# Batch 1's queries turned by the DMA crossbar instead of TensorE, with batch 2's loads and the work around them re-ordered

## The chip, the cores and the metric

The kernel runs on one core of a Trainium2 chip. The metric is device time in microseconds (us), lower is better. Before the change it is 317.51 us, the median of 3 runs (317.42 to 317.64). A profile's own span, from the first to the last instruction, is 1.8 to 2.1 us shorter than the device time of the same run. All timed runs told of here are of the fast state, except two single runs whose state cannot be told (slow1 and slow2).

## The reference

Linear attention over 8 batches, then a SwiGLU block over all 4,608 tokens:

```python
# q, k, v: (batch 8, heads 8, seq 576, dim 64), float32
q_s = softmax(q, over dim);  k_s = softmax(k, over seq)
kv  = einsum('bhsd,bhse->bhde', k_s, v)
x   = einsum('bhsd,bhde->bhse', q_s, kv)      # -> (4608, 512)
g, val = x @ w_gate, x @ w_val                 # (512, 1536) each
out = (g * sigmoid(g) * val) @ w_out           # (1536, 512)
```

## The kernel before

The SwiGLU block fills TensorE; the attention of batch b+1 is slipped in between its products. Batch 1 is the exception: its attention stands alone between the twelve units of batch 0 (`m_unit`, 576 tokens) and the first chunk of the main loop (448 tokens). I call the stretch from batch 0's first output product to the first output product of the next chunk **the passage**. Every head group G (two in a batch) goes through the same steps: load q, k, v; Exp on ScalarE; row sums, reciprocal and multiply on VectorE (`norm_sum`, `norm_mul`); a transpose of the normalised q; K^T V with the sums of k (`kv_...`), scaled (`scale_...`); and x = q^T times that (`x_...`), copied into `xt`, which the units read.

```python
    ld = ctx.enter_context(tc.tile_pool(name="ld", bufs=3))     # 3 buffers each of q, k, v
    ff = ctx.enter_context(tc.tile_pool(name="ff", bufs=3))     # 3 buffers of Silu's result
    psp = ctx.enter_context(tc.tile_pool(name="psp", bufs=8, space=bass.MemoryType.PSUM))
    # ... cut
    def turn_pe(b, G, i):          # by TensorE: 5 + 4 transposes into one PSUM bank each
        # ... cut
            nc.tensor.transpose(out=tp[:, j * 128:(j + 1) * 128], in_=s["qs"][:, t, :], identity=ident)
    def turn_out(b, G, i, eng):    # and a copy out of PSUM
        # ... cut
    def turn_dma(b, G):            # by the DMA crossbar; batches 2 to 7 use it
        s = st[b, G]
        qt = s["qt"] = at.tile([128, T, 128], BF16, tag="qt", name="qt")
        nc.sync.dma_start_transpose(out=qt, in_=s["qs"].rearrange("p t c -> p (t c)"))
    # ... cut
    def m_unit(c0, n, m, by_part=False):     # gate and value products, Silu, product
        # ... cut: two PSUM banks, 4 + 4 matmuls
            nc.scalar.activation(out=sg[:, 0:w_], in_=g_ps[:, 0:w_], func=AF.Silu)
            nc.vector.tensor_mul(hr[:, m, r:r + w_], sg[:, 0:w_], u_ps[:, 0:w_])
    # ... cut
        load_batch(1, w_dma[-3], by_group=True)
        load_batch(2)
        for m in range(MT):
            m_unit(0, S, m, by_part=(m == 0))
        exp_of("q", 1, 0); exp_of("k", 1, 0); exp_of("q", 1, 1)
        cast_v(1, 0); cast_v(1, 1)                      # GpSimd
        norm_sum(1, 0); norm_mul(1, 0); norm_sum(1, 1)  # VectorE
        o_out(0, o_mm(0), nc.scalar); o_out(1, o_mm(1), nc.scalar)
        exp_of("k", 1, 1)
        # turn, K^T V, scale and x of group 0, then of group 1, round o_mm(2) and o_mm(3)
        # ... cut
        exp_of("q", 2, 0); exp_of("q", 2, 1)
        x_one(1, 1)
        o_out(3, p)
        exp_of("k", 2, 0); exp_of("k", 2, 1)

        for ci, (c0, n) in enumerate(chunks):
            # ... cut: in the first chunk, in front of units 1 to 4: cast, norm_sum,
            # norm_mul and turn_dma of batch 2
                if att and m == 8:
                    kv_both(b)
                    scale_both(b)
                    if b + 1 < B:
                        load_batch(b + 1)
                m_unit(c0, n, m)
                if att and m == 9:
                    x_both(b)
```

(Several calls are put on one line here.) In the traces ScalarE loads a table whenever it goes from Exp to Silu or back (1.28 us each), so an Exp among Silus costs two table loads. And the program has eight PSUM banks (`bufs=8`), handed round among all products: a product waits until the last reader of its bank is done.

The softmax here doesn't subtract the row's maximum and nothing guards it: scores larger than these inputs give would overflow.

Of the kernel before, what the change touches and what calls it, by code (L numbers as in the profile page):

```python
# [15 lines left out]
def kernel(  # L16
# [30 lines left out]
    def bank(name):  # L47
        return psp.tile([128, 512], FP32, tag="ps", name=name)
# [34 lines left out]
    def load_batch(b, after=None, by_group=False):  # L83
        qkv = (("q", q), ("k", k), ("v", v))
        if by_group:
            order = [(w, s, G) for G in range(NG) for w, s in qkv]
        else:
            order = [(w, s, G) for w, s in qkv for G in range(NG)]
        for w, s, G in order:
            load(w, s, b, G, after=after)  # L90
            after = None
# [40 lines left out]
    def norm_sum(b, G, pieces=((0, T),)):  # L132
        s = st[b, G]
        eq2 = s["eq"].rearrange("p t h d -> p (t h) d")
        rs = at.tile([128, 2 * T], FP32, tag="rs", name="rs")
        first = None
        for t0, t1 in pieces:
            i = nc.vector.reduce_sum(  # L138
                out=rs[:, 2 * t0:2 * t1], in_=eq2[:, 2 * t0:2 * t1, :], axis=mybir.AxisListType.X
            )  # L140
            first = first or i
        rr = s["rr"] = at.tile([128, 2 * T], FP32, tag="rr", name="rr")
        nc.vector.reciprocal(out=rr, in_=rs)
        return first

    def norm_mul(b, G, pieces=((0, T),), engs=None):
        s = st[b, G]
        eq2 = s["eq"].rearrange("p t h d -> p (t h) d")
        qs = s["qs"] = at.tile([128, T, 128], BF16, tag="qs", name="qs")
        for (t0, t1), eng in zip(pieces, engs or (nc.vector, nc.vector)):  # L150
            n = 2 * (t1 - t0)
            eng.tensor_mul(  # L152
                qs[:, t0:t1, :].rearrange("p t (h d) -> p (t h) d", d=64),
                eq2[:, 2 * t0:2 * t1, :],
                s["rr"][:, 2 * t0:2 * t1].to_broadcast([128, n, 64]),
            )
# [126 lines left out]



    def m_unit(c0, n, m, by_part=False):
        ms = slice(m * 128, (m + 1) * 128)
        parts = [(c0, n)] if n <= 512 else [(c0, 320), (c0 + 320, n - 320)]
        gu = []
        for nm in ("g_ps", "u_ps"):  # L290
            ps = [bank(nm) for _ in parts]
            gu.append(ps)
        steps = [(a, kk, i) for a in range(2) for kk in range(KT) for i in range(len(parts))]
        if by_part:
            steps.sort(key=lambda a: (a[2], a[0], a[1]))
        for a, kk, i in steps:
            c, w_ = parts[i]
            nc.tensor.matmul(  # L298
                out=gu[a][i][:, 0:w_], lhsT=(wg, wv)[a][:, kk, ms], rhs=xt[:, kk, c:c + w_],
                start=(kk == 0), stop=(kk == KT - 1),  # L300
            )
        for g_ps, u_ps, (c, w_) in zip(gu[0], gu[1], parts):
            r = c % RING
            sg = ff.tile([128, 512], BF16, tag="sg", name="sg")
            nc.scalar.activation(out=sg[:, 0:w_], in_=g_ps[:, 0:w_], func=AF.Silu)  # L305
            nc.vector.tensor_mul(hr[:, m, r:r + w_], sg[:, 0:w_], u_ps[:, 0:w_])  # L306
# [8 lines left out]
            )  # L315
            engs[half].dma_start(out=dst, in_=o_sb[64 * half:64 * half + 64, c0:c1])

    def o_mm(j):
        o_ps = bank("o_ps")
        r0 = (j * 128) % RING  # L320
        for m in range(MT):
            nc.tensor.matmul(  # L322
                out=o_ps, lhsT=hr[:, m, r0:r0 + 128], rhs=wo[:, m, :],
                start=(m == 0), stop=(m == MT - 1),
            )
        return o_ps
# [26 lines left out]
    with tc.manual_schedule():  # L353
# [98 lines left out]
        x_out(0, 1, 1, xp1[1], (nc.scalar, nc.vector))  # L452

        load_batch(1, w_dma[-3], by_group=True)
        load_batch(2)

        for m in range(MT):
            m_unit(0, S, m, by_part=(m == 0))
# [5 lines left out]
        cast_v(1, 1)  # L464
        norm_sum(1, 0)
        norm_mul(1, 0)
        norm_sum(1, 1)
        o_out(0, o_mm(0), nc.scalar)
        o_out(1, o_mm(1), nc.scalar)
        exp_of("k", 1, 1)  # L470
        turn_pe(1, 0, 0)
        turn_pe(1, 0, 1)
        turn_out(1, 0, 0, nc.scalar)
        turn_out(1, 0, 1, nc.scalar)
        kv_one(1, 0)
        scale_one(1, 0, (nc.vector, nc.vector))
        norm_mul(1, 1)
        p = o_mm(2)
        x_one(1, 0)
        o_out(2, p)  # L480
        turn_pe(1, 1, 0)
        turn_pe(1, 1, 1)
        turn_out(1, 1, 0, nc.scalar)
        turn_out(1, 1, 1, nc.scalar)
        kv_one(1, 1)
        scale_one(1, 1, (nc.vector, nc.vector))
        p = o_mm(3)
        exp_of("q", 2, 0)
        exp_of("q", 2, 1)
        x_one(1, 1)  # L490
        o_out(3, p)
        exp_of("k", 2, 0)
        exp_of("k", 2, 1)


        chunks = [(S, 448)] + [(c, 512) for c in range(1024, n_tok, 512)]
        for ci, (c0, n) in enumerate(chunks):
            b = ci + 2
            jo = 4 * ci
            att = b < B  # L500
            final = ci == len(chunks) - 1
            for m in range(MT):
                if ci == 0:
                    if m == 1:
                        cast_v(b, 0)
                        cast_v(b, 1)
                        norm_sum(b, 0)
                    elif m == 2:
                        norm_mul(b, 0)
                        turn_dma(b, 0)  # L510
                    elif m == 3:
                        norm_sum(b, 1)
                    elif m == 4:
                        norm_mul(b, 1)
                        turn_dma(b, 1)
                elif m == 3:
                    if att:
                        exp_of("q", b, 0)
                        exp_of("q", b, 1)
                        norm_sum(b, 0)  # L520
                    o_unit(jo)
                    if att:
                        norm_mul(b, 0)
                        turn_dma(b, 0)
                    o_unit(jo + 1)
                    if att:
                        norm_sum(b, 1)
                elif m == 4 and att:
                    norm_mul(b, 1)
                    turn_dma(b, 1)  # L530
                elif m == 7:
                    if att:
                        exp_of("k", b, 0)
                        exp_of("k", b, 1)
                        cast_v(b, 0)
                        cast_v(b, 1)
                    o_unit(jo + 2)
                    if not final:
                        o_unit(jo + 3)
                if att and m == 8:  # L540
                    kv_both(b)
                    scale_both(b)
                    if b + 1 < B:
                        load_batch(b + 1)
                m_unit(c0, n, m)
                if att and m == 9:
                    x_both(b)
        o_unit(jo + 3)
# [34 lines left out]
```

## Time and profile before

| 317.51 us, profiled span 316.0 us | us |
|---|---|
| TensorE busy in the whole span | 304.7 (96%) |
| the passage, 39.19 to 79.09 | 39.90, TensorE busy 39.20 |
| rest of the program after the passage | 236.89 |

The page's line of busy time, and the first line of the chain that ended last:

```profile
...
PE 304.7 (96%) x1865; PEld 152.0 (48%) x1894; DVE 163.2 (52%) x277; ACT 147.6 (47%) x218; POOL 28.0 (9%) x35
...
PE 88%; DMA 4%; DVE 3%; ACT 2%; issue 1%; POOL 1%; SPq 0%; DVEq 0%
...
```

TensorE is the limit. The busy time of each engine in the passage (busy us, then the number of instructions, for each engine; granted TensorE clock, DMA share and rate at the end):

```profile
...
core 0: us, PE busy (x) PEld busy (x) DVE busy (x) ACT busy (x) POOL busy (x), PEclk, DMA share, GB/s
39.19:79.09 39.90, 39.20 (x289) 19.80 (x291) 27.59 (x49) 24.92 (x39) 5.29 (x5) 1.00 0.80 276
...
```

TensorE's timeline in the passage (start, length, what, how many; in brackets idle time before it and who ended it; lengths overlap a little, so read the starts):

```profile
...
44.62 0.68 PE L166 MATMUL tp<-ident,qs 128*128 128x128 bf16 x9
45.23 0.70 PE L191 MATMUL kv<-vb,ek 64*128 64x129 bf16 x18
...
49.08 0.68 PE L166 MATMUL tp<-ident,qs 128*128 128x128 bf16 x9
49.69 0.70 PE L191 MATMUL kv<-vb,ek 64*128 64x129 bf16 x18
...
53.02 0.44 PE L220 MATMUL xp<-qt,kn 64*64 64x320 bf16 x8
53.39 0.55 PE L298 MATMUL g_ps<-xt,wg 128*128 128x448 bf16 x2
54.14 0.54 PE L298 MATMUL g_ps<-xt,wg 128*128 128x448 bf16 x2 [0.20 <-ACT xt L111]
...
65.96 1.22 PE L191 MATMUL kv<-vb,ek 64*128 64x129 bf16 x36
...
70.25 0.69 PE L267 MATMUL xp<-qt,kn 64*64 64x512 bf16 x16
...
```

The `tp` lines are the 18 transposes that the change removes: from 44.62 to 45.23 and from 49.08 to 49.69, 0.61 us each. The bracket before 54.14 is the first unit waiting for the copy of x. The first unit's steady start is 53.76, the second unit's 55.27 less the period of 1.51. K^T V of batch 2 starts at 65.96 and x of batch 2 at 70.25 without any wait.

ScalarE's timeline of the same stretch:

```profile
...
53.97 2.23 ACT L124 ACTIVATE ek<-k 128x1152 bf16<-128x1152 f32 x2
56.22 1.28 ACT L305 ACT_TABLE_LOAD   x1
57.51 1.42 ACT L305 ACTIVATE sg<-g_ps 128x448 bf16<-128x448 f32 x3
59.26 0.54 ACT L305 ACTIVATE sg<-g_ps 128x448 bf16<-128x448 f32 x1 [0.33 <-PE g_ps L298]
60.84 0.54 ACT L305 ACTIVATE sg<-g_ps 128x448 bf16<-128x448 f32 x1 [1.04 <-DVE hr L306]
62.64 0.54 ACT L305 ACTIVATE sg<-g_ps 128x448 bf16<-128x448 f32 x1 [1.25 <-DVE hr L306]
...
```

All four exponentials of batch 2 are done before the first unit's Silu at 57.51; the sixth Silu starts at 62.64. After that ScalarE stands idle in front of each Silu until VectorE has done a product (`<-DVE hr`), because VectorE alternates these products with the normalisation of batch 2.

### The profile page before, as it was taken

Reading aid. Unit: us, or ns where it says so; the run is one execution under the profiler, and the core shown is the slowest. Engines: PE = TensorE matmul, PEld = TensorE weight load, DVE = VectorE, ACT = ScalarE, POOL = GpSimd, SP = SyncE. Lnnn points to the kernel's source line nnn. Section 1 sums busy time; section 2 is a strip of 40 time slices with the busy share of each in tenths; the row PEclk is TensorE's granted clock in tenths of the full one; section 3 lists DMA queues with packets and bytes.
Section 4 is the critical chain, followed back from the end, with each engine's and each line's share of the span. In section 5 each row is a group of like instructions: output and inputs, shape, how many; then the busy total and the mean of one; then the engine's idle time right before and its main releaser. Section 6 shows DMA issues by size and latency. Waiting matters only on the chain.

```text
span 316.0 us, 4856 instructions
## 1 busy us (share of the span) xinstructions
PE 304.7 (96%) x1865; PEld 152.0 (48%) x1894; DVE 163.2 (52%) x277; ACT 147.6 (47%) x218; POOL 28.0 (9%) x35
## 2 busy tenths in 40 slices
PE   6799999999999999999999999999999999999994
PEld 2477744554444444544454444544454444444443
DVE  3834476685754566455835492639354333423421
ACT  4743488634663465447354637355743113312300
POOL 2930021100200020002000200020000000000000
PEclk9999999999999999999999999999999999999999
DMA  7999999269246806490629253944310202020124
GB/s 269 183 204 207 296 393 391 68 160 364 50 91 179 338 17 128 112 394 11 141 68 352 97 110 66 322 162 103 66 41 0 65 3 66 0 68 3 31 68 102
DMA packets 39304, 45.75 MB, mean 145 GB/s; under 512 B 16368, under 2 KB 23024, under 8 KB 39280
## 3 DMA queue, kind: packets, MB, share of 16 engines
q1 hardware_dynamic: 32480, 39.99, 42.0%
q0 software_dynamic: 6640, 5.31, 10.9%
q8 instruction: 15, 0.25, 0.3%
q10 hardware_dynamic: 160, 0.13, 0.2%
q14 instruction: 9, 0.07, 0.1%
HBM read 37.75 MB, written 9.44 MB: 149 GB/s over the span
## 4 chain that ended last, share of the span: by engine, by line
PE 88%; DMA 4%; DVE 3%; ACT 2%; issue 1%; POOL 1%; SPq 0%; DVEq 0%
PE g_ps L298 29%; PE u_ps L298 29%; PE o_ps L322 25%; PE kv L191 3%; DMA wv<-in_moe_w_val_dram 2%; DMA k<-in_k_dram 2%; DVE rs L138 1%; PE xp L267 1%; DVE qs L152 1%; PE o_ps L342 1%; ACT L124 1%; ACT eq L124 1%; POOL v L361 0%; PE tp L166 0%; POOL v L358 0%
## 5 line engine op out<-in xcount | busy, mean ns | idle before, releaser
L305 ACT ACTIVATE sg<-g_ps 128x512 bf16<-128x512 f32 (+2 forms) x120 | 65.1, 554 | 139.1 <-PE g_ps L298 120.7
L306 DVE TENSOR_TENSOR hr<-sg,u_ps 128x512 bf16<-128x512 bf16 (+2 forms) x120 | 74.5, 630 | 87.8 <-PE u_ps L298 80.4
L298 PE MATMUL g_ps<-xt,wg 128*128 128x512 bf16 (+2 forms) x469 | 110.0, 358 | 1.0 <-ACT xt L111 0.2
L298 PE MATMUL u_ps<-xt,wv 128*128 128x512 bf16 (+2 forms) x468 | 109.8, 357 | 1.2 <-DMA wv<-in_moe_w_val_dram 0.5
L322 PE MATMUL o_ps<-wo,hr 128*128 128x512 bf16 x414 | 93.0, 379 | 0.4 <-issue 0.2
L298 PEld LDWEIGHTS <-wv 128*128 128x128 bf16 x480 | 46.9, 98 | 47.2 <-DMA wv<-in_moe_w_val_dram 0.9
L298 PEld LDWEIGHTS <-wg 128*128 128x128 bf16 x480 | 45.8, 98 | 45.3 <-issue 0.7
L322 PEld LDWEIGHTS <-hr 128*128 128x128 bf16 x420 | 40.9, 98 | 49.1
L113 DVE COPY o_sb<-o_ps 128x512 f32<-128x512 f32 x33 | 22.4, 680 | 39.2 <-PE o_ps L322 37.3
L127 POOL CAST vb<-v 128x1152 bf16<-128x1152 f32 x14 | 16.0, 1146 | 174.3 <-DMA v<-in_v_dram 111.8
L138 DVE TENSOR_REDUCE rs<-eq 128x18 f32<-128x1152 bf16 (+2 forms) x18 | 21.7, 1214 | 13.2 <-ACT eq L124 13.2
L152 DVE TENSOR_TENSOR qs<-eq,rr 128x1152 bf16<-128x1152 bf16 (+2 forms) x18 | 22.1, 1237 | 0.1
L124 ACT ACTIVATE eq<-q 128x1152 bf16<-128x1152 f32 (+2 forms) x18 | 18.1, 1050 | 4.5 <-DMA q<-in_q_dram 4.4
L124 ACT ACTIVATE ek<-k 128x1152 bf16<-128x1152 f32 x16 | 18.0, 1158 | 0.3 <-DMA k<-in_k_dram 0.2
L305 ACT ACT_TABLE_LOAD x12 | 15.4, 1283 | 0.2
L124 ACT ACT_TABLE_LOAD x11 | 14.1, 1283 | 0.2
L388 PE MATMUL idle<-zero 128*128 128x512 bf16 x20 | 6.1, 459 | 3.0 <-DVE rs L138 1.8
L191 PE MATMUL kv<-vb,ek 64*128 64x129 bf16 x252 | 8.7, 217 | 0.0
L191 PEld LDWEIGHTS <-ek 64*128 64x128 bf16 x252 | 7.3, 94 | 2.7 <-ACT sg L305 2.1
L275 ACT CAST xt<-xp 128x512 bf16<-128x512 f32 x12 | 6.4, 588 | 3.6 <-PE xp L267 3.6
L276 DVE CAST xt<-xp 128x512 bf16<-128x512 f32 x12 | 7.7, 683 | 0.0
L347 ACT COPY o_sb<-o_ps 128x128 f32<-128x128 f32 x2 | 0.5, 265 | 13.3 <-DVE o_sb L346 13.3
(46 smaller groups left out, 70.2 us busy)
## 6 DMA issues: line engine op xcount, KB each, us to landing
q<-in_q_dram SPq DMA_DIRECT2D x16, 576.0 KB, 5.6
k<-in_k_dram SPq DMA_DIRECT2D x16, 576.0 KB, 7.3
out_dram<-o_sb SPq DMA_DIRECT2D x70, 128.0 KB, 2.3
v<-in_v_dram SPq DMA_DIRECT2D x14, 576.0 KB, 9.0
wo<-in_moe_w_out_dram POOLq DMA_DIRECT2D x4, 384.0 KB, 16.3
wg<-in_moe_w_gate_dram POOLq DMA_DIRECT2D x2, 384.0 KB, 9.7
wv<-in_moe_w_val_dram POOLq DMA_DIRECT2D x2, 384.0 KB, 10.7
wg<-in_moe_w_gate_dram POOLq DMA_DIRECT2D x1, 512.0 KB, 13.7
```

The source lines that it names most:

```text
L113: eng.tensor_copy(out=out, in_=in_)
L124: nc.scalar.activation(out=e[:, t0:t1], in_=src[:, t0:t1], func=AF.Exp)
L127: nc.gpsimd.tensor_copy(out=vbs[G][:, :, 0:128].rearrange("p t (h d) -> p t h d", d=64), in_=raw["v", b, G].rearrange("p h (t d) -> p t h ...
L138: i = nc.vector.reduce_sum(out=rs[:, 2 * t0:2 * t1], in_=eq2[:, 2 * t0:2 * t1, :], axis=mybir.AxisListType.X)
L152: eng.tensor_mul(qs[:, t0:t1, :].rearrange("p t (h d) -> p (t h) d", d=64), eq2[:, 2 * t0:2 * t1, :], s["rr"][:, 2 * t0:2 * t1].to_broadca ...
L191: nc.tensor.matmul(out=kv[g][:, c:c + 129], lhsT=ek_of(b, G, g, t), rhs=vbs[G][r, t, 0:129], start=(t == 0), stop=(t == T - 1),)
L275: nc.scalar.copy(out=xt[:, 2 * G, c0:c0 + 512], in_=main[G][0])
L276: nc.vector.tensor_copy(out=xt[:, 2 * G + 1, c0:c0 + 512], in_=main[G][1])
L298: nc.tensor.matmul(out=gu[a][i][:, 0:w_], lhsT=(wg, wv)[a][:, kk, ms], rhs=xt[:, kk, c:c + w_], start=(kk == 0), stop=(kk == KT - 1),)
L305: nc.scalar.activation(out=sg[:, 0:w_], in_=g_ps[:, 0:w_], func=AF.Silu)
L306: nc.vector.tensor_mul(hr[:, m, r:r + w_], sg[:, 0:w_], u_ps[:, 0:w_])
L322: nc.tensor.matmul(out=o_ps, lhsT=hr[:, m, r0:r0 + 128], rhs=wo[:, m, :], start=(m == 0), stop=(m == MT - 1),)
```

## The change

Its intent: take the 18 transposes and their four PSUM copies from TensorE and ScalarE, let the crossbar do them in time that K^T V and output products cover, and keep the SyncE queue free for them by issuing batch 2's loads around and behind them instead of far ahead. K^T V and x of batch 1 move apart, half an output product between them; the first unit reads the four blocks of x in two groups so that it can start on the first; and the last exponential of batch 2 moves into the first chunk.

```diff
         load_batch(1, w_dma[-3], by_group=True)
-        load_batch(2)
@@
         norm_mul(1, 0)
+        turn_dma(1, 0)
+        load("q", q, 2, 0)
         norm_sum(1, 1)
+        norm_mul(1, 1)
+        turn_dma(1, 1)
+        load("q", q, 2, 1)
+        for what, src in (("k", k), ("v", v)):
+            for G in range(NG):
+                load(what, src, 2, G)
         o_out(0, o_mm(0), nc.scalar)
         o_out(1, o_mm(1), nc.scalar)
         exp_of("k", 1, 1)
-        turn_pe(1, 0, 0)
-        turn_pe(1, 0, 1)
-        turn_out(1, 0, 0, nc.scalar)
-        turn_out(1, 0, 1, nc.scalar)
         kv_one(1, 0)
-        scale_one(1, 0, (nc.vector, nc.vector))
-        norm_mul(1, 1)
+        scale_one(1, 0, (nc.scalar, nc.scalar))
         p = o_mm(2)
+        kv_one(1, 1)
+        o_out(2, p)
+        scale_one(1, 1, (nc.vector, nc.vector))
+        p = o_mm(3, m1=MT // 2)
+        exp_of("q", 2, 0)
         x_one(1, 0)
-        # ... cut: turn, K^T V, scale of group 1, o_mm(3), exponentials of q
+        o_mm(3, p, m0=MT // 2)
         x_one(1, 1)
         o_out(3, p)
+        exp_of("q", 2, 1)
         exp_of("k", 2, 0)
-        exp_of("k", 2, 1)
@@
                     elif m == 4:
                         norm_mul(b, 1)
                         turn_dma(b, 1)
+                    elif m == 5:
+                        exp_of("k", b, 1)
@@
-                m_unit(c0, n, m)
+                m_unit(c0, n, m, by_group=(ci == 0 and m == 0))
```

More of the change, by code (lines that the diff above doesn't have):

```diff
@@ L282, in x_both, with m_unit @@
             )
-    def m_unit(c0, n, m, by_part=False):
+    def m_unit(c0, n, m, by_part=False, by_group=False):
         ms = slice(m * 128, (m + 1) * 128)
@@ L295, in m_unit @@
             steps.sort(key=lambda a: (a[2], a[0], a[1]))
+        if by_group:
+            steps.sort(key=lambda a: (a[1] // 2, a[0], a[1]))
         for a, kk, i in steps:
@@ L316, in store, with o_mm @@
             engs[half].dma_start(out=dst, in_=o_sb[64 * half:64 * half + 64, c0:c1])
-    def o_mm(j):
-        o_ps = bank("o_ps")
+    def o_mm(j, o_ps=None, m0=0, m1=MT):
+        if o_ps is None:
+            o_ps = bank("o_ps")
         r0 = (j * 128) % RING
-        for m in range(MT):
+        for m in range(m0, m1):
             nc.tensor.matmul(
@@ L470 @@
         exp_of("k", 1, 1)
-        turn_pe(1, 0, 0)
-        turn_pe(1, 0, 1)
-        turn_out(1, 0, 0, nc.scalar)
-        turn_out(1, 0, 1, nc.scalar)
         kv_one(1, 0)
-        scale_one(1, 0, (nc.vector, nc.vector))
-        norm_mul(1, 1)
+        scale_one(1, 0, (nc.scalar, nc.scalar))
         p = o_mm(2)
-        x_one(1, 0)
-        o_out(2, p)
-        turn_pe(1, 1, 0)
-        turn_pe(1, 1, 1)
-        turn_out(1, 1, 0, nc.scalar)
-        turn_out(1, 1, 1, nc.scalar)
-        kv_one(1, 1)
-        scale_one(1, 1, (nc.vector, nc.vector))
-        p = o_mm(3)
-        exp_of("q", 2, 0)
-        exp_of("q", 2, 1)
+        kv_one(1, 1)
[3 more added lines that the diff above has]
+        exp_of("q", 2, 0)
+        x_one(1, 0)
+        o_mm(3, p, m0=MT // 2)
         x_one(1, 1)
         o_out(3, p)
+        exp_of("q", 2, 1)
         exp_of("k", 2, 0)
-        exp_of("k", 2, 1)
         chunks = [(S, 448)] + [(c, 512) for c in range(1024, n_tok, 512)]
```

## The prediction

> **What bounds the kernel now.** TensorE. The page shows it busy 304.7 of 316.0 us (96%), and the chain of waits puts 88% of the span on it; granted clock 0.998. The change touches only 39 to 74 us, the passage from batch 0's twelve units to the first chunk of the main loop. The sums over stretches give TensorE 13.75 of 14.19 us busy in 39.20-53.39 and 20.31 of 20.51 in 53.39-73.90. Little idle time can be won; what can go is work.
>
> **What the change removes** (timeline of TensorE). The 18 transposes of batch 1 and the waits around them: 0.86 us before 45.23 and 0.82 us before 49.69. Also a 0.2-0.3 us hole before the third output product, and about 0.35 us before the first chunk unit (0.2 us of it a wait for ScalarE's copy of x), which the order by group should hide. Together about 2.0 us. ScalarE loses four copies out of PSUM (2.4 us).
>
> **What it adds and moves.** Two crossbar transposes: the two of batch 2 took 1.3 us to issue and 3.3 us to land on a quiet queue. Here the queue is full: from 39 to 55 us the DMA engines are saturated at 390 GB/s and loads land in order of issue, one per 1.5 us (the second v of batch 1 at 46.62). The Trainium skill, "DMA: Bandwidth & Descriptors", section "Queues, rings and completion order", says that descriptors are consumed in ring order on each engine; these landings agree. My estimates: first transpose issued 44.6, behind v, landed about 48.5, in time (needed 49.8). Batch 2's first q load is issued at 46 instead of 36.3 and lands about 50.5 instead of 48.1. Second transpose issued about 48.2, landed 51.6 to 52.3; TensorE wants it at 51.5. The second q load lands about 53.8 instead of 49.7, the first k load about 55.3.
>
> **How much stays.** ScalarE runs the exponential of that first q load ahead of x's copies, so x of the first half is ready only about 52.5 to 52.9. The first chunk unit's steady start moves from 53.76 to about 52.7: 1.0, not 2.0 us. ScalarE then waits for the second q and first k loads, so its first Silu slips from 57.5 to about 57.8. In the first chunk VectorE alternates Silu products with batch 2's normalisation, a chain that starts from that Silu; today batch 2's second transposed tile lands at 69.26 and TensorE uses it at 70.25, 1.0 us of slack. Chain 0.3 later: the gain is capped at about 0.7 us there. The fourth exponential, moved into the chunk, costs ScalarE two more table loads (1.28 us each), mostly in time it spends waiting for VectorE. Later chunks only shift.
>
> **Prediction.** 316.8 us, range 316.0 to 317.9. Faster by over 2%: 0.01; within 2%: 0.97; slower by over 2%: 0.02.
>
> **What would show each step.** Right: no TensorE transposes after 20 us; crossbar transposes issued near 44.6 and 48.2, landing near 48.5 and 52; a TensorE hole under 1 us before the second x product or the first chunk unit, and one of a few tenths before batch 2's x product near 69.5; first Silu near 57.8; after that only a shift of 0.7 us. Wrong: x of batch 1 waiting over 1 us for a transpose; the q load landing after 51.5; or a first Silu before 57.5, which would let 1.0 us or more through.
>
> **What would make it wrong.** Crossbar transposes far slower in a busy queue, or holding up the loads behind them (a loss of 1 to 3 us); loads quicker than I reckon, or PSUM banks dealt out so that TensorE never meets VectorE's chain (a gain of 1.3 to 1.7 us).

## The result, and the profile after

The changed kernel takes 318.57 us (median of 4 runs, 318.07 to 319.35) against 317.57 us of before (317.42 to 318.08). Ratios are the mean time of one kernel's runs over that of the other's runs of the same rounds, so not quite the ratio of these medians: 1.0034, 95% interval 1.0016 to 1.0052. Two later measurements of the same kernel gave 1.0016 (1.0004 to 1.0028) and 1.0039 (0.9999 to 1.0079). Over all 15 runs its median is 318.39 us, so it loses about 0.8 us. I had forecast a gain of 0.7.

The page of the changed kernel (of its fastest run of the first four, 318.07 us):

```profile
...
PE 305.0 (96%) x1848; PEld 151.8 (48%) x1876; DVE 162.1 (51%) x275; ACT 148.7 (47%) x218; POOL 29.3 (9%) x35
...
PE 84%; DMA 7%; DVE 2%; ACT 2%; issue 2%; POOL 2%; SPq 0%; DVEq 0%; ACTq 0%
...
```

The passage after, under the same columns as before:

```profile
...
38.91:79.49 40.58, 38.46 (x271) 18.88 (x272) 26.80 (x47) 26.01 (x39) 6.24 (x5) 1.00 0.91 284
...
```

The work did leave: TensorE is busy 38.46 us in the passage instead of 39.20. But the passage has grown from 39.90 to 40.58 us, so its idle time went from 0.70 to 2.12. After the passage nothing differs (236.78 us against 236.89). Here is TensorE's timeline; each code line has moved by two or three (L298 is now L300, L322 is L325):

```profile
...
44.19 0.70 PE L191 MATMUL kv<-vb,ek 64*128 64x129 bf16 x18
44.81 2.76 PE L325 MATMUL o_ps<-wo,hr 128*128 128x512 bf16 x11
48.30 0.70 PE L191 MATMUL kv<-vb,ek 64*128 64x129 bf16 x18 [0.72 <-POOL vb L127]
48.93 1.47 PE L325 MATMUL o_ps<-wo,hr 128*128 128x512 bf16 x6
50.33 0.44 PE L220 MATMUL xp<-qt,kn 64*64 64x320 bf16 x8
50.70 1.47 PE L325 MATMUL o_ps<-wo,hr 128*128 128x512 bf16 x6
52.10 0.44 PE L220 MATMUL xp<-qt,kn 64*64 64x320 bf16 x8
52.47 0.55 PE L300 MATMUL g_ps<-xt,wg 128*128 128x448 bf16 x2
...
65.39 0.23 PE L191 MATMUL kv<-vb,ek 64*128 64x129 bf16 x1 [0.45 <-DVE hr L308]
66.39 1.21 PE L191 MATMUL kv<-vb,ek 64*128 64x129 bf16 x35 [0.77 <-ACT sg L307]
...
70.66 0.69 PE L267 MATMUL xp<-qt,kn 64*64 64x512 bf16 x16
...
```

Up to 52.47 the change did what it was made for: no transposes, x of both halves without a wait, the first unit steady from its first matmul. (One wait is new: 0.72 us for GpSimd's cast of v, in front of the second K^T V.) Then, in front of K^T V of batch 2, TensorE waits twice. Counted from the start of the passage (39.19 before, 38.91 after):

| us from the passage's start | before | after | difference |
|---|---|---|---|
| first unit, steady | 14.57 | 13.56 | -1.01 |
| first Silu of the chunk | 18.32 | 19.22 | +0.90 |
| K^T V of batch 2, first matmul | 26.77 | 26.48 | -0.29 |
| second matmul of it | 26.78 | 27.47 | +0.70 |
| x of batch 2 | 31.06 | 31.75 | +0.69 |
| end of the passage | 39.90 | 40.58 | +0.68 |

ScalarE's timeline says who was late:

```profile
...
56.83 1.28 ACT L307 ACT_TABLE_LOAD   x1
58.13 1.85 ACT L307 ACTIVATE sg<-g_ps 128x448 bf16<-128x448 f32 x4
61.46 0.54 ACT L307 ACTIVATE sg<-g_ps 128x448 bf16<-128x448 f32 x1 [1.48 <-DVE hr L308]
62.02 1.28 ACT L124 ACT_TABLE_LOAD   x1
63.31 1.16 ACT L124 ACTIVATE ek<-k 128x1152 bf16<-128x1152 f32 x1
64.50 1.28 ACT L307 ACT_TABLE_LOAD   x1
65.79 0.98 ACT L307 ACTIVATE sg<-g_ps 128x448 bf16<-128x448 f32 x2
...
```

The first Silu starts at 58.13; four Silus run until 59.98, a fifth at 61.46. Then come a table load, the moved exponential (63.31) and a table load back, and the sixth Silu cannot start before 65.79. It ends at 66.33, and the second matmul of K^T V starts at 66.39. In the program as built (this is read from the build, not from the trace), K^T V's second accumulator sits in the PSUM bank of the sixth unit's gate product, which this Silu reads, and its first in the bank of the fourth unit's value product, which VectorE's fourth product reads until 65.33; that product is late because its chain starts from the late first Silu.

The landings of the DMAs, from the trace's own records:

| landed at, us | before | after | predicted |
|---|---|---|---|
| v of batch 1, second half | 46.62 | 45.83 | about 46.6 |
| first turned tile | | 48.26 | 48.5 |
| first q of batch 2 | 48.12 | 50.21 | 50.5 |
| second turned tile | | 51.31 | 51.6 to 52.3 |
| second q of batch 2 | 49.68 | 54.13 | 53.8 |
| first k of batch 2 | 51.12 | 55.63 | 55.3 |
| second k of batch 2 | 52.63 | 57.13 | |

### The profile page after: what moved, and what is told of

It is laid out like the page before. It is cut to its first block, busy times and chain, and to the rows that moved or that the text cites. A ratio compares the mean times of both kernels' runs of the same rounds, so it can differ in the third digit from the quotient of the medians.

```text
span 316.3 us, 4822 instructions
## 1 busy us (share of the span) xinstructions
PE 305.0 (96%) x1848; PEld 151.8 (48%) x1876; DVE 162.1 (51%) x275; ACT 148.7 (47%) x218; POOL 29.3 (9%) x35
## 3 DMA queue, kind: packets, MB, share of 16 engines
q1 hardware_dynamic: 34848, 40.58, 43.6%
## 4 chain that ended last, share of the span: by engine, by line
PE 84%; DMA 7%; DVE 2%; ACT 2%; issue 2%; POOL 2%; SPq 0%; DVEq 0%; ACTq 0%
PE g_ps L300 28%; PE u_ps L300 27%; PE o_ps L325 25%; DMA v<-in_v_dram 3%; PE kv L191 2%; DMA wv<-in_moe_w_val_dram 2%; DMA k<-in_k_dram 2%; DVE rs L138 1%; PE xp L267 1%; PE o_ps L345 1%; ACT L124 1%; POOL vb L127 1%; ACT sg L307 0%; POOL v L364 0%; DVE qs L152 0%
## 5 line engine op out<-in xcount | busy, mean ns | idle before, releaser
L300 PE MATMUL g_ps<-xt,wg 128*128 128x512 bf16 (+2 forms) x469 | 110.0, 357 | 0.8 <-issue 0.2
L300 PE MATMUL u_ps<-xt,wv 128*128 128x512 bf16 (+2 forms) x468 | 109.9, 357 | 0.7
L325 PE MATMUL o_ps<-wo,hr 128*128 128x512 bf16 x415 | 93.4, 379 | 0.2
L300 PEld LDWEIGHTS <-wv 128*128 128x128 bf16 x480 | 46.8, 98 | 46.9 <-DMA wv<-in_moe_w_val_dram 0.4
L300 PEld LDWEIGHTS <-wg 128*128 128x128 bf16 x480 | 45.8, 98 | 45.1 <-issue 1.0
L325 PEld LDWEIGHTS <-hr 128*128 128x128 bf16 x420 | 40.9, 98 | 49.1 <-issue 0.2
L127 POOL CAST vb<-v 128x1152 bf16<-128x1152 f32 x14 | 17.3, 1233 | 173.4 <-DMA v<-in_v_dram 133.2
L152 DVE TENSOR_TENSOR qs<-eq,rr 128x1152 bf16<-128x1152 bf16 (+2 forms) x18 | 21.8, 1222 | 0.1
L391 PE MATMUL idle<-zero 128*128 128x512 bf16 x20 | 7.3, 525 | 3.2 <-DVE rs L138 2.0
L350 ACT COPY o_sb<-o_ps 128x128 f32<-128x128 f32 x2 | 0.5, 265 | 13.3 <-DVE o_sb L349 13.3
```

The source lines that it names most:

```text
L127: nc.gpsimd.tensor_copy(out=vbs[G][:, :, 0:128].rearrange("p t (h d) -> p t h d", d=64), in_=raw["v", b, G].rearrange("p h (t d) -> p t h ...
L152: eng.tensor_mul(qs[:, t0:t1, :].rearrange("p t (h d) -> p (t h) d", d=64), eq2[:, 2 * t0:2 * t1, :], s["rr"][:, 2 * t0:2 * t1].to_broadca ...
L300: nc.tensor.matmul(out=gu[a][i][:, 0:w_], lhsT=(wg, wv)[a][:, kk, ms], rhs=xt[:, kk, c:c + w_], start=(kk == 0), stop=(kk == KT - 1),)
L325: nc.tensor.matmul(out=o_ps, lhsT=hr[:, m, r0:r0 + 128], rhs=wo[:, m, :], start=(m == 0), stop=(m == MT - 1),)
L391: i = nc.tensor.matmul(out=idle, lhsT=zero[:, 0:128], rhs=zero, start=True, stop=True)
```

## The experiments

Eighteen experiments ran (four of them on a kernel that had run before). For each I give the edit against the changed kernel (unless said otherwise), what was expected of it, what came, and what follows. "Passage" is the length defined above, read from the one trace that each kernel leaves; times are of all its runs. A passage is the sharper measure here, because the end of the program, 236.8 us, is the same everywhere but in one trace; but one trace is one run, and not always a typical one: those of k_m4, k_m4_x_m10 and all3 are of their kernels' fastest runs, that of k_early of its slowest.

### The changed kernel again

No edit.

> The changed kernel unaltered, to see whether its first profile is typical. Two theories of its loss. A (chain and bank): about 1.2 us are won by 53 us and given back in the first chunk, in the two waits of kv of batch 2 (0.45 us for VectorE's fourth product, 0.77 us for the sixth Silu, which the moved exponential and its two table loads hold up, and with it a PSUM bank) and then in x of batch 2, which follows the landing of the second transposed tile (70.44) by 0.2 us. Expected under A: ratio to before 1.002 to 1.005, the same two waits in the profile, 1.0 to 1.3 us together. B (chance): the loss comes from a slow landing of the crossbar transposes in a busy queue that differs from run to run; then a second profile shows a wait for a transposed tile in the passage before 53 us, and the times scatter by more than 1 us.

318.10 us (median; 317.95 to 318.88) against 317.65 of before. The passage took 40.45 us, with 0.80 us of idle time before K^T V for the Silu again and no wait over 0.3 us for a turned tile:

```profile
...
66.42 1.21 PE L191 MATMUL kv<-vb,ek 64*128 64x129 bf16 x35 [0.80 <-ACT sg L307]
...
```

The larger of theory A's two waits was there again. The other, for VectorE, was not: v had landed 1.25 us later than in the first trace (47.08), so TensorE started the first unit 14.04 us into the passage, a gain of 0.53 instead of 1.01, and came to K^T V that much later. The ratio, 1.0016, lies just under the 1.002 that A had set. B did not explain this trace. The times scattered by 0.9 us.

### The moved exponential one unit earlier

```diff
                         turn_dma(b, 1)
-                    elif m == 5:
                         exp_of("k", b, 1)
```

> Only the fourth exponential of batch 2 is moved, from before unit 5 to before unit 4, where ScalarE has 1.5 us to spare. Theory A: the wait of kv for Silu (0.77 us) goes, the one for VectorE (about 0.45) stays, and TensorE then stands still about 0.7 us in front of x of batch 2 for the second transposed tile, which still lands near 70.4: gain against the changed kernel 0.0 to 0.3 us only. Rival: if the held PSUM bank is the whole cause, 0.7 us or more are gained.

ScalarE in this kernel:

```profile
...
58.03 1.85 ACT L307 ACTIVATE sg<-g_ps 128x448 bf16<-128x448 f32 x4
59.90 1.28 ACT L124 ACT_TABLE_LOAD   x1
61.19 1.16 ACT L124 ACTIVATE ek<-k 128x1152 bf16<-128x1152 f32 x1
62.37 1.28 ACT L307 ACT_TABLE_LOAD   x1
63.67 0.98 ACT L307 ACTIVATE sg<-g_ps 128x448 bf16<-128x448 f32 x2
...
```

and TensorE, K^T V and x of batch 2:

```profile
...
65.56 1.22 PE L191 MATMUL kv<-vb,ek 64*128 64x129 bf16 x36
...
69.84 0.73 PE L267 MATMUL xp<-qt,kn 64*64 64x512 bf16 x16
...
```

The exponential now sits in the pause of ScalarE behind the fourth Silu. The sixth Silu is over by 64.65 instead of 66.33, although K^T V uses the same pair of banks, and neither wait of K^T V is left. The missing wait for VectorE is not the repair's doing: v landed late here too (47.92), and the first unit started 14.16 us into the passage, much as in again. Again is therefore the trace to compare with, and against it the second matmul of K^T V comes 0.96 us earlier (26.38 against 27.34 us into the passage): that is the wait for the Silu. The passage took 39.54 us, 0.9 to 1.0 us less than the two traces of the changed kernel. That is more than my 0.0 to 0.3: I had expected x to wait about 0.7 us for the second turned tile of batch 2, near 70.4 us, but that landed at 69.83 here and x started at 69.84. Why it landed earlier is told below. So in the traces the held bank is the larger part of the loss. The times do not show it: 318.17 us (317.28 to 318.52), a median no lower than the changed kernel's 318.10 on the same chip, and a mean of 317.99 against 318.24. The trace is of the fastest of the five runs.

### x of batch 2 one unit later, alone and with the other

```diff
-                if att and m == 9:
+                if att and m == (10 if ci == 0 else 9):
                     x_both(b)
```

> Only x of batch 2 is moved, from after unit 9 to after unit 10 in the first chunk, so that its transposed tile has 1.5 us more. Theory A: kv waits as before (1.2 us in all), nothing waits at x, and the time is that of the changed kernel to within 0.3 us. Rival: if the late transposed tile alone is the cause, 0.7 us or more are gained.

318.50 us (318.00 to 320.32), no gain, as theory A said; both waits of K^T V were there. But the passage took 41.80 us, for another reason: its second turned tile was issued 0.8 us later than in the first trace (see the next section), x of batch 1 waited 1.15 us for it and the first Silu came 20.4 us into the passage.

> Both moves. Theory A: each alone gives at most 0.3 us, both together 0.7 to 1.1 us against the changed kernel, that is about 317.3 to 317.8 against 317.5 of before; only the wait of kv for VectorE (about 0.45 us) is left in the first chunk. Rival (each cost is independent of the other): the gain is the sum of the two single gains.

317.79 us (316.92 to 318.51), passage 39.60 us. The mean, 317.77, is 0.5 us under the changed kernel's on the same chip and level with before (ratio 1.0007, interval 0.9994 to 1.0020). That the two repairs only work together, which theory A had said, does not show in the traces, where the passage is no shorter than with the first alone; the times cannot decide it.

### The changed kernel without its fourth exponential in the chunk

```diff
         exp_of("k", 2, 0)
+        exp_of("k", 2, 1)
@@
-                    elif m == 5:
-                        exp_of("k", b, 1)
```

> The changed kernel with its fourth exponential back in front of the first chunk, so without the two extra table loads. Theory A (chain): k lands near 57.1 us, so the first Silu slips from 58.1 to about 59.6, and the chain of VectorE behind it by the same; the passage from the first output product to that of the first chunk takes about 1 us more than with the change (40.5), so 41 to 42 us. Rival (the two table loads are the cost): the passage takes about 1 us less.

319.99 us (318.67 to 320.83), 1.6 us over the changed kernel's median, and a passage of 43.38 us. Undoing the move that holds the bank makes things worse, because the first Silu now waits for the second k as well, which lands at 58.05 in this trace; it comes 21.8 us into the passage, and TensorE runs out of banks in the fifth unit:

```profile
...
PE g_ps L300 <- ACT sg L307: 2.0, 1, 2.0
...
```

About 0.9 us of the 43.38 (an estimate from again2 in the next section) have another cause, a lost meeting of VectorE with GpSimd, which delays everything in this trace. Even without it the passage is longer than with the change, and the ratio to before, 1.0078 (1.0054 to 1.0101), lies above every one of the changed kernel's. The two table loads alone are therefore not the cost. The cost is that the first Silu depends on loads which the new order brings late; the moved exponential was put into the chunk to soften just that, one unit too late.

### The meeting of VectorE and GpSimd

In the changed kernel, the second multiply of batch 1 (VectorE) and the cast of its second v (GpSimd) often become ready at the same moment. The Trainium skill, "SBUF — State Buffer", section "Who interferes with whom", says that a VectorE instruction with two SBUF inputs, as this multiply is, contends with a GpSimd instruction that reads SBUF, that the shared ports are an exclusive lock, and that the order of issue decides who blocks. The traces agree. Here are the multiply and the cast of the first trace of the changed kernel,

```profile
...
45.88 1.36 DVE L152 TENSOR_TENSOR qs<-eq,rr 128x1152 bf16<-128x1152 bf16 x1
...
```

```profile
...
45.88 2.36 POOL L127 CAST vb<-v 128x1152 bf16<-128x1152 f32 x1 [3.30 <-DMA v<-in_v_dram]
...
```

and of another run of it (again2), where the cast came first:

```profile
...
45.95 2.32 DVE L152 TENSOR_TENSOR qs<-eq,rr 128x1152 bf16<-128x1152 bf16 x1
...
```

```profile
...
45.91 1.15 POOL L127 CAST vb<-v 128x1152 bf16<-128x1152 f32 x1 [3.30 <-DMA v<-in_v_dram]
```

Alone they take 1.36 and 1.15 us; whichever loses stretches to 2.1 to 2.4. The multiply lost in four of the 20 traces (again2, x_m10, k_early and half, 2.12 to 2.34 us). When it loses, the crossbar transpose behind it, the q load behind that and the first Silu are all late by 0.8 us. In again2 that gave a passage of 41.39 us. I took the meeting away by giving the cast to ScalarE:

```diff
         cast_v(1, 0)
-        cast_v(1, 1)
@@
         exp_of("k", 1, 1)
+        nc.scalar.copy(out=vbs[1]..., in_=raw["v", 1, 1]...)      # cut
         kv_one(1, 0)
```

> The changed kernel, with the cast of the second v of batch 1 made by ScalarE (after the exponential of k, where it stands idle about 1.2 us) instead of by GpSimd. Theory C: in the changed kernel that cast and VectorE's second normalising multiply meet at the same moment, and whichever comes second stands still until the other is done; in one run VectorE lost 0.75 us so, and with it the issue of the second crossbar transpose, the q load behind it and the first Silu (1.2 us). Without the meeting: no wait of kv for GpSimd (0.7 to 1.3 us before), the multiply takes 1.36 us, the waits of kv of batch 2 in the first chunk stay; the slowest of the runs comes down by a microsecond, mean 0.2 to 0.6 us under the changed kernel's. Rival: the scatter comes from the DMA queue alone; then the spread of the runs stays above 1 us and the mean moves by less than 0.2 us.

It got worse: 319.46 us (318.16 to 322.74). In the trace (passage 40.72 us) v landed at 47.38, as late as in again and k_m4, and ScalarE, which now had the cast in its own order of work, stood waiting for it. That run took 318.37 us, so it does not explain the 319.46. Theory C's forecast for the scatter is refuted, although the collision itself is real.

> All three repairs: exponential of k before unit 4, x of batch 2 after unit 10, and the cast on ScalarE. If theories A and C both hold: every run between 316.7 and 317.6, median about 317.1, and under before's by 0.3 to 0.7 us; no wait of TensorE over 0.5 us in the passage. If the scatter is the DMA queue's, the median stays at 317.6 to 317.9, as with the first two repairs alone.

318.49 us (317.11 to 319.79). Its one trace has the shortest passage of any kernel with two crossbar transposes, 39.17 us, and its slowest run is 2.7 us slower than its fastest. Its forecast, every run under 317.6, failed; the median is no better than the change's.

To see a slow run, cast_act ran twice more for its trace alone.

> The kernel cast_act once more, for a trace of a slow run: its six runs went from 318.16 to 322.74 us, and only the trace of the second fastest is known. Theory D: the scatter is that of the landings in the SyncE queue round the two crossbar transposes. In a slow run v of batch 1, a transposed tile or a q load behind it lands more than 1 us later than in the known trace (47.4, 48.5, 51.6, 54.1 us), TensorE waits for it before 56 us or for a Silu in the first chunk, and everything outside 39 to 80 us takes as long as ever. Rival: the lost time lies elsewhere, in the main loop or before 39 us. A run under 318.5 us tells nothing.

> The same once more, with the same expectations as the run before: at 4 slow runs in 6 the chance that at least one of the two shows a slow run is about 0.9.

318.64 and 318.47 us: not slow enough to show what happens in a run of 320 or 322 us. Both passages (40.48 and 40.68) look like the first. What makes the slowest runs remains open.

### The queue

The change without the crossbar (TensorE transposes at the places of the new order, everything else kept):

```diff
-        turn_dma(1, 0)
         load("q", q, 2, 0)
@@
-        turn_dma(1, 1)
         load("q", q, 2, 1)
@@
         exp_of("k", 1, 1)
+        turn_pe(1, 0, 0); turn_pe(1, 0, 1)
+        turn_out(1, 0, 0, nc.scalar); turn_out(1, 0, 1, nc.scalar)
         kv_one(1, 0)
@@      # and the same for group 1 in front of o_mm(3)
```

> The change without its crossbar: batch 1's queries turned by TensorE and copied by ScalarE again, at the places of the new order; all moves of the change are kept (loads, split output product, order by group, exponentials). The passage then pays 1.2 us for 18 transposes again but no load waits behind a transpose in the queue: first Silu about 1.3 us earlier against the start of the passage than in the changed kernel, no wait of kv of batch 2. Theory: the order alone is worth 0.2 to 0.5 us against before (317.1 to 317.4), so the crossbar is what costs. Rival: the moved exponential costs by itself; then kv of batch 2 waits for a Silu here too, and the time is 318 or more.

317.63 us (317.40 to 317.64), ratio 1.0001: level with before, and all five runs within 0.24 us. No wait of K^T V of batch 2, although the exponential sits in front of unit 5 here too: the first Silu came 18.24 us into the passage, the loads not being held up. The passage took 39.60 us; the rest took 0.5 us longer in that trace. That half microsecond lies behind TensorE's last product (4.50 us to the end of the span, 3.9 to 4.1 in the other 19 traces), in the last stores; why is open. So the 0.2 to 0.5 us that I expected of the order alone did not show in the time. The rival (the moved exponential costs by itself) is refuted: it costs only together with late loads. Part of the slack here is TensorE's own: with the transposes it starts the first unit 0.55 us later than in the first trace of the change, but the first Silu comes 0.98 us earlier, which is the larger share.

Next, the loads back where they were, ahead of both transposes:

```diff
         load_batch(1, w_dma[-3], by_group=True)
+        load_batch(2)
@@       # and the six loads behind the transposes removed
```

> The change with batch 2's loads issued where they stood before, ahead of both transposes in the SyncE queue. Theory (one queue, served in order): the transposes wait until those six loads have landed (about 55.6 us), so they land near 57.5 and 59.5 us instead of 48.3 and 51.3, x of batch 1 waits for them, and the time is 5 to 7 us over the changed kernel's. Rival (the engines share out by packet between transfers in flight): the transposes land by 51 to 53 us and the loss is under 2 us.

324.61 us (both runs within 0.1 us), 6.2 us over the changed kernel's median. TensorE's x of batch 1:

```profile
...
56.41 0.69 PE L220 MATMUL xp<-qt,kn 64*64 64x320 bf16 x8 [5.83 <-DMA qt<-qs]
...
```

The last of batch 2's loads landed at 55.35 us and the turned tiles at 56.37 and 57.41, strictly after it. That is what the Trainium skill, "DMA: Bandwidth & Descriptors", section "Queues, rings and completion order", says of descriptors consumed in ring order. In one queue a transpose waits for every load issued ahead of it, and every load issued behind waits for it.

So I tried the other hardware queue: transposes issued by ScalarE, loads early on SyncE, the exponential in front of unit 4, and x's copies ahead of the exponential of q.

```diff
-        nc.sync.dma_start_transpose(out=qt, ...)
+        eng.dma_start_transpose(out=qt, ...)      # nc.scalar for batch 1
```

> Crossbar transposes of batch 1 kept, but issued on ScalarE's queue, batch 2's loads issued early as before the change, exponential of k before unit 4 and x's copies ahead of the exponential of q. If the cost is the place in the SyncE queue (transposes wait for loads, loads for transposes): the q loads land at 48 to 51 us again, the first Silu comes under 18.5 us after the start of the passage (19.1 to 19.2 with the change), the transposes land within 6 us of their issue although the engines are full, and the time is 316.7 to 317.3, with a spread under 0.6 us. Rival: a crossbar transpose among running loads is slow or irregular from any queue; then tiles land later than 53 us, x of batch 1 waits for them, and the time is 318 or more with a spread over 1 us.

326.36 us (325.44 to 326.99), the worst of all:

```profile
...
PE xp L220 <- DMA qt<-qs: 7.3, 1, 7.3
...
```

The tiles landed 13.3 and 11.3 us after their issue. The DMA queues between 50.5 and 54.5 us show why (packets, MB, share of the engines):

```profile
...
q1 hardware_dynamic: 644, 1.39, 88.9%
q10 hardware_dynamic: 645, 0.17, 18.8%
...
```

q1 carries the loads and q10 the transposes. The counts, 644 against 645, fit engines that take one packet from each in turn. A packet of the loads has 2,304 bytes and one of the transposes 256, so q10 moved an eighth of the bytes and its two transposes crawled for as long as there were loads. The same section of that page says that the engines go round between queues at packet granularity, and its section "Issuing engines are not separate DMA queues" that issuing from several engines saves only the sequencer's issue time. This run agrees with both, and adds the price for the side with the small packets.

### TensorE's instruction fetches

TensorE's program of about 3,800 instructions is fetched in packets of 16,384 bytes on a queue of their own (the page lists q8 with kind "instruction"; its 15 packets before the change fit that number). The Trainium skill, "Runtime: NRT & Kernel Launch", section "Instruction fetch mechanics", gives blocks of 256 instructions and calls the cost of crossing into the next one "mostly hidden". That is said of the engine that fetches; a crossbar transpose beside the fetch did pay. I compared every crossbar transpose of batches 2 to 7, in all 20 traces, with the fetches:

| fetch during the transpose | transposes | issue to landing, us |
|---|---|---|
| none | 212 | 3.17 to 3.45 |
| begun less than 0.2 us after the issue, or before it | 12 | 3.17 to 3.41 |
| begun 0.5 to 1.5 us after the issue | 10 | 3.58 to 4.66 |
| begun 2.6 to 2.9 us after the issue | 6 | 3.20 to 4.85 |

In the changed kernel's first trace one fetch begins at 67.53, 0.87 us after the issue of the second transpose of batch 2, which then lands 3.78 us after it. In k_m4 K^T V is not held up, TensorE reaches that place of its program earlier, the fetch comes at 66.27, before the transpose is issued at 66.60, and the tile lands in 3.23 us. At 3.8 us it would have held x back by about 0.6: that is most of why k_m4's trace gained more than I had allowed it. The fetch at 45.37 comes during the first transpose of batch 1.

To move the fetches I lengthened the warm-up of TensorE by 48 or 84 instructions, with narrower products of about the same duration:

```diff
-        spin(8)                  # 8 products of 512 columns
+        spin(32, w=128)          # 32 products of 128 columns; 84: the third spin as well
```

> The kernel with the first two repairs, and TensorE's program lengthened by 48 instructions in its warm-up (32 products of 128 columns for 8 of 512), so that the 16 KB fetches of its instructions come about 5 us earlier in the passage: the one at 45.1 us moves to about 40, away from the first crossbar transpose. Theory F (fetches): first transpose lands 3.2 to 3.5 us after its issue (3.6 to 4.3 so far), the runs draw together (spread under 0.7 us against 1.6) and the mean falls by 0.3 us or more. Rival: landings and spread stay as they are, 316.9 to 318.5.

317.10 us (316.58 to 317.42); before on the same chip had 317.62 (317.18 to 319.13), ratio 0.9977, interval 0.9955 to 0.9999. The fetch moved from 45.12 to 42.86 us and the first transpose landed 3.66 us after its issue (3.73 without the padding, so hardly earlier; the fetch had been meant to move by 5 us and moved by 2.3). The passage, 39.53 us, is no shorter than the 39.60 without padding, and the spread of 0.84 us misses the 0.7. The unpadded kernel had 317.79 and a ratio of 1.0007 on another chip. The direction of the times fits theory F, but the passage, the chips and the intervals do not let me call it shown.

So the pair was run on one chip, for the change alone, with the kernel before padded too as a control.

> The changed kernel unaltered, third measurement, as the partner of the next run on the same chip: 318.0 to 319.4, spread over 0.8 us, both the first crossbar transpose of batch 1 and the second of batch 2 landing 3.5 us or more after their issue with a fetch in between.

> The changed kernel with 84 more TensorE instructions in the warm-up (56 products of 128 columns for 14 of 512), nothing else. Theory F: the fetches at 45.3 and 67.5 us come before the transposes; the second of batch 2 lands 3.2 us after its issue, the first of batch 1 about 0.4 us earlier; the waits of kv of batch 2 stay (1.0 to 1.3 us in all); mean 0.2 to 0.5 us under that of its partner and a smaller spread. Rival (fetches do not matter to the time): mean and spread equal to the partner's within 0.2 us.

> The same 84 instructions in the kernel before, as a control: it has no crossbar transpose in the passage, so the time should be that of before within 0.15 us. If it falls as far as after_pad does, the warm-up itself is the gain and not the place of the fetches.

again2: 318.43 us (317.94 to 322.27). after_pad: 318.31 us (318.02 to 318.73). before_pad: 317.46 us (317.30 to 318.39), the time of before (317.61; 316.92 to 319.58). In after_pad the two transposes landed 3.33 and 3.21 us after their issue, where again2's took 4.28 and 3.58: the fetches' effect on landings is as forecast. The time is not: without again2's one outlier of 322.27 the means differ by 0.06 us. The waits of K^T V (0.90 and 0.32 us) are all still there in after_pad. Its passage took 41.17 us: with the new warm-up it began 0.5 us earlier (at 38.40), but the first k of batch 2 landed at 55.70, by the clock as before, and TensorE waited away inside the passage what it had gained ahead of it. So the fetches delay single transposes by 0.4 to 1.5 us, but they are not the cause of the change's loss. Whether they make the slow outliers is open: here before itself had a run of 319.58.

### One crossbar transpose instead of two

If a second transpose holds back the loads, use only the first. The edit takes k_m4, gives the second group back to TensorE (9 transposes in front of its K^T V), issues all of batch 2's loads right behind the one transpose, and copies x before the exponential of q:

```diff
         turn_dma(1, 0)
         load("q", q, 2, 0)
+        load("q", q, 2, 1)
         norm_sum(1, 1)
         norm_mul(1, 1)
-        turn_dma(1, 1)
-        load("q", q, 2, 1)
@@
         p = o_mm(2)
+        turn_pe(1, 1, 0); turn_pe(1, 1, 1)
+        turn_out(1, 1, 0, nc.scalar); turn_out(1, 1, 1, nc.scalar)
         kv_one(1, 1)
@@
-        exp_of("q", 2, 0)
         x_one(1, 0)
+        exp_of("q", 2, 0)
```

> Crossbar for the first half of batch 1 alone, TensorE for the second half (9 transposes, 0.62 us); all of batch 2's loads right behind the one crossbar transpose; exponential of k before unit 4. Theory G (the second crossbar transpose is what costs: it holds back the q load behind it and all that follows, and its own landing is irregular): the q and k loads land at 50.2, 51.7 and 53.2 us, the first Silu comes near 17.3 us after the start of the passage, nothing waits in the first chunk, the passage takes 38.7 to 39.2 us (39.9 before, 40.5 with the change), the time is 316.3 to 316.9 and the spread under 0.6 us. Rival: one crossbar transpose among the loads is enough for the scatter; then the spread stays over 1 us.

317.04 us (316.45 to 317.14) against 317.62 of before: ratio 0.9969, interval 0.9949 to 0.9989. That is just outside the forecast. The passage took 39.66 us in its trace, in which TensorE waited 0.7 us for VectorE's multiply, which had lost its meeting with the cast (2.31 us), and the first q landed only at 50.96. Against k_m4 this kernel differs in three things at once (one crossbar transpose fewer, the order of the loads, x's copies before the exponential), so it tests theory G as a whole and not the second transpose by itself.

> The kernel half with the same 48 instructions more in the warm-up. Theory F: the one crossbar transpose lands 0.4 us earlier than in half and the spread is smaller; the time is the same or up to 0.3 us less. Rival: no difference.

316.54 us (316.29 to 317.63, a wider spread than half's and not the smaller one forecast), ratio 0.9966, interval 0.9943 to 0.9988. Its passage took 38.90 us, the shortest of all 20 traces. The one transpose landed 3.31 us after its issue (3.81 in half), q and k of batch 2 at 50.13, 51.68 and 53.20, and the first Silu came 17.69 us into the passage, 0.6 us earlier than before the change. TensorE:

```profile
...
47.41 0.67 PE L166 MATMUL tp<-ident,qs 128*128 128x128 bf16 x9
48.29 0.70 PE L191 MATMUL kv<-vb,ek 64*128 64x129 bf16 x18 [0.22 <-POOL vb L127]
...
52.47 0.55 PE L300 MATMUL g_ps<-xt,wg 128*128 128x448 bf16 x2
...
```

The 9 transposes are back at 47.41, and the first unit still starts at 52.47, as in the changed kernel, because they fill the time in which that one waited for the cast of v (0.72 us; 0.22 here): the second K^T V starts at 48.29 here and at 48.30 there. So taking these 9 transposes from TensorE had gained nothing in that trace. After this nothing waits. half and half_pad beat the kernel before, each by an interval that leaves out 1; the changed kernel was not run beside them, but its own ratios all lie above 1. Between the two the intervals cannot choose.

## Why the prediction was wrong

- **What bounds the kernel, and that only the passage changes**: right. The rest of the program took 236.8 us before and after.
- **The gain up to the first unit**: right. Forecast 1.0 us ("The first chunk unit's steady start moves from 53.76 to about 52.7"), measured 1.01 against the passage's start in the first trace (0.53 in again, 0.85 in again2).
- **The landings**: right to within about 0.3 us for the first turned tile and all three loads, and 0.3 us early for the second tile, in the first trace.
- **The first Silu**: mis-sized. Forecast 0.3 us late (57.5 to 57.8), measured 58.13, and 0.90 us later against the passage's own start, which was 0.28 us earlier in this trace. The delay was known, but I compared it with a clock, not with TensorE, which arrives sooner.
- **The step that failed**: "The fourth exponential, moved into the chunk, costs ScalarE two more table loads (1.28 us each), mostly in time it spends waiting for VectorE." It does not fit into that time. ScalarE's pause is 1.5 us, the three instructions take 3.7. The sixth Silu ends at 66.33, 1.4 us after TensorE could have started K^T V, and that Silu's gate product holds the bank which K^T V needs. I had counted ScalarE's time and the chain of VectorE, but not who holds a PSUM bank. In place of a slack of 1.0 us at x of batch 2, the chunk had two waits in front of K^T V. Between the starts of their matmuls they cost 0.52 us (for VectorE's fourth product) and 0.99 us (for the Silu and its bank), a smaller hole at 58.72 another 0.19, together 1.70 us. -1.01 + 1.70 is the +0.69 seen at x.
- **"The gain is capped at about 0.7 us there"**: the place was right, the size was not. A gain of 1.0 was over-paid by 1.7.
- **The scatter** of the changed kernel was not foreseen. One cause is shown in traces: the meeting of multiply and cast, which lengthens the passage by about 0.9 us when the multiply loses (41.39 against 40.45 and 40.58). Fetches shift single landings. The slowest runs of the changed kernel and of cast_act (319.35 to 322.74 us) were never caught in a trace, and their cause stays open.

That the order costs nothing without the crossbar is shown by pe_turn. That the held bank is what TensorE waits for is shown by k_m4's trace beside again's, and not by k_m4's times, whose median did not fall. That late loads are behind it is shown by k_early and pe_turn from both sides. So the loss of 0.8 us as a whole is traced to the crossbar among the loads; how much of it the bank makes up in an ordinary run is open.

## What to carry to other kernels

Moving work from the bound engine into a queue is paid in that queue: a crossbar transpose among loads delays every load behind it, and on a second queue it is served one small packet for each large one. When an operation moves into a pause of an in-order engine, compare its whole length, table loads included, with the pause, and then ask which buffers or PSUM banks the instructions behind it hold, and who will want them. If the bound engine arrives earlier, every wait that was just met before becomes a wait, so measure slack from the new arrival and not from the old clock.

## What the Trainium skill lacked or had wrong

- "DMA: Bandwidth & Descriptors" says that queues are served in turn by packet; it lacks what this means for a crossbar transpose beside loads on another queue. Measured: 645 packets of 256 bytes for 644 of 2,304, and 11.3 to 13.3 us to land instead of 3.2.
- "Advanced Engine Details and Errata", section "X-Bar Transpose (TRN2)", calls transposes "as fast as regular DMAs" (and expects about 90% of a copy). Measured in loads_first: the second of two queued transposes of 294,912 bytes landed 1.04 us after the first (one pair in one trace), about 284 GB/s, where loads of 589,824 bytes landed 1.5 us apart, about 393 GB/s: 72%.
- "Runtime: NRT & Kernel Launch" calls the cost of an instruction fetch mostly hidden, for the engine that fetches. Measured: all 10 crossbar transposes in which a fetch began 0.5 to 1.5 us after the issue landed in 3.58 to 4.66 us, the 212 without one in 3.17 to 3.45. No page says that a fetch delays a crossbar transpose.
